# Next pass's x and second-layer weights held back by one-column writes on GpSimd, in a banded-attention and two-layer fp32 kernel

## The chip, the cores and the metric

The kernel runs on one core of a Trainium2 chip. The metric is the device time of one execution in microseconds (us); the median of three runs of the kernel before is 960.06 us (960.06, 960.06, 960.84). One further execution was profiled. Engines are named as in the profile: PE is TensorE's matmuls and PEld its weight loads, DVE is VectorE, ACT is ScalarE, POOL is GpSimd, SP is SyncE, which here only issues DMAs. Each engine runs its own list of instructions in order.

## The reference

q, k, v and the output are float32, the weights are float64. For 4 batches and 8 heads of 576 positions and 64 channels, a causal attention with a band of 64 positions is computed; its output is read as x with 2304 tokens and 512 channels; then come two feed-forward layers:

```
scores = where(0 <= i - j < 64, q @ k.T / 8, -1e9)
x = softmax(scores) @ v                                # 2304 x 512
g = x @ w_gate; x = (g * sigmoid(g) * (x @ w_val)) @ w_out     # 1536 wide
h = x @ w_in;  out = maximum(0.01 * h, h) @ w_out2             # 2048 wide
```

The float64 weights arrive as pairs of 32-bit words and are made float32 on the chip.

## The kernel before, in words

**Numbers.** Each float32 operand of a product is split into a high part (a rounded copy, written by ACT) and a low part (operand minus high part, written by DVE, or by POOL for the activations). Every product then takes three matmuls: high·high, high·low and low·high. `split` (lines 273 to 275) does it for weights and for x, `halves` (lines 635 to 644) for the second layer's activations, with the low part on POOL (line 644).

**First layer.** Tokens go in six blocks (`BLOCKS`, line 51): block 0 and block 5 are 512 tokens wide, blocks 1 to 4 are 320 wide. A block has 12 steps (`step1`, line 539), one for each 128 columns of w_gate and w_val (block 0 has 24, as its tokens go in two halves of 256): product `pg` on PE, tanh on ACT (line 549), `th` on DVE (line 550), product `pv`, `th` again on DVE (line 557), high part g0 on ACT (line 559), low part g1 on POOL (line 560), and then, one step later, `out1` adds g times w_out into four PSUM accumulators. `pg` and `pv` share two PSUM buffers. Attention for the next block runs between the steps, from a plan of slots; a step is three slots, so blocks 1 to 5 have 36 slots each and block 5 begins at slot 216. At the end of a block its x goes to a DRAM buffer, x2d (line 537).

**The second layer's weights** are prepared during the first layer. There are 16 portions of this work, 8 times `ready2` (line 311) and 8 times `ready2o` (line 324), in turn. Each loads two 512 KB pieces (`narrow`, line 257: a DMA by SP into a `raw` buffer, then ACT line 265 and DVE lines 266 and 267 make float32 of it), takes four sums or differences on DVE, splits its seven half-tiles in four calls of `keep2` and stores them in DRAM. All of it goes through the pool `rawp` with three buffers. The portions are handed out at equal distances over slots 92 to 216 (lines 583 to 585), that is, before block 5.

**Second layer.** The two products are done with seven-product (Strassen-Winograd) schemes on halves, over three passes of 768 tokens; a pass has 8 units, so there are 24 units (`units`, line 340; the loop is at line 731). A unit has seven products of 6 matmuls of 384 columns (`product`, line 617: 42 matmuls in the PSUM tiles pw, px, py), whose sums DVE forms (lines 765, 790, 801 to 824), a leaky ReLU on ACT (line 749), the splits of seven operands, and 63 matmuls of 256 columns for the unit before it (`part_y`, line 662), which DVE adds into SBUF sums (line 659; line 657 copies instead of adding in the first unit of a pass). At the end of a pass `finish` and `total` (line 693) put these sums together and store them.

**The next pass's x** comes from x2d. `load_x2(i, part)` (line 397) loads two tiles and issues four subtractions and five splits, `finish_x2` (line 419) four more splits: for the two parts together 8 subtractions and 14 splits, so 22 DVE instructions a pass. It is called for pass 0 in steps 4, 6 and 7 of block 5, and for passes 1 and 2 at the end of units 2 and 4 and in unit 7 of the pass before.

**What sets the order.** The program does not give each engine's order directly. `prio(slot)` sets a priority for what is written next, and a scheduler with a timing model of its own builds the order of each engine from data dependences, free buffers and these priorities. An instruction that is written late with a late priority is still placed early when its data and buffers are there and its engine is free in that model.

Of the kernel before, what the change touches and what calls it, by code (L numbers as in the profile page):

```python
# [27 lines left out]
def banded_attention_moe_moe(  # L28
# [228 lines left out]
    def narrow(src):  # L257

        raw = rawp.tile([P, 512, 2], I32, tag="raw", name="raw")
        flat = raw.rearrange("p f two -> p (f two)")  # L260
# [47 lines left out]
    def two(t):  # L308
        return t.rearrange("p (k n) -> p k n", k=2)

    def ready2(fp):
        x, y = (two(narrow(w2_in[:, f * 2 * P:f * 2 * P + 2 * P].rearrange("(c p) f -> p c f", p=P)))
# [11 lines left out]
    def ready2o(fp):  # L324
        x, y = (two(narrow(w2_out[f * P:f * P + P, :])) for f in (2 * fp, 2 * fp + 1))
# [66 lines left out]
    def split_x2(i, part, k, src):  # L392
        t = two(entry((0, 1, 2, 3, 8, 9), 2 * HALF, place[i][k, part]))
        split(t[:, 0], t[:, 1], src)
        X2[i, part, k] = t

    def load_x2(i, part):

        t0 = PASSES[i]
        r = []  # L400
        for c in (part, part + 2):
            r.append(rawp.tile([P, 2 * HALF], F32, tag="raw", name="x2raw"))
            nc.sync.dma_start(out=r[-1], in_=x2d[c * P:(c + 1) * P, t0:t0 + 2 * HALF])
        b11, b12 = r[0][:, 0:HALF], r[0][:, HALF:2 * HALF]
        b21, b22 = r[1][:, 0:HALF], r[1][:, HALF:2 * HALF]
        t1, t2, t3 = (inb[:, HALF * j:HALF * j + HALF] for j in range(3))
        t4 = (e0, pT)[part].rearrange("p t j -> p (t j)")[:, 0:HALF]
        nc.vector.tensor_tensor(t1, b12, b11, op=ALU.subtract)
        nc.vector.tensor_tensor(t2, b22, t1, op=ALU.subtract)
        split_x2(i, part, A11, b11)  # L410
        split_x2(i, part, S2, t2)
        split_x2(i, part, S1, t1)
        nc.vector.tensor_tensor(t3, b22, b12, op=ALU.subtract)
        nc.vector.tensor_tensor(t4, b21, t2, op=ALU.subtract)
        split_x2(i, part, A12, b21)
        split_x2(i, part, S3, t3)
        x2src[i, part] = (b22, t4)

    def finish_x2(i):
        for j, k in enumerate((S4, A22)):  # L420
            for part in range(2):
                split_x2(i, part, k, x2src[i, part][j])
# [116 lines left out]
    def step1(slot, blk, cols, f, first, last):  # L539
# [20 lines left out]
        nc.gpsimd.tensor_tensor(g[1][:, :n], th, f32(g[0][:, :n]), op=ALU.subtract)  # L560
        reach(slot + 1.4)
# [21 lines left out]
    begin2 = FIRST[1] + 20  # L583
    every = (FIRST[NBLK - 1] - begin2) / NP2
    todo2 = [(begin2 + every * (i + h / 2), fn, i) for i in range(NP2) for h, fn in enumerate((ready2, ready2o))]
    for blk in range(1, NBLK):
        for f in range(NF1):
# [6 lines left out]
            if blk == NBLK - 1:  # L594
                if f in (4, 6):
                    prio(slot - 6)
                    load_x2(0, f // 2 - 2)
                if f == 7:
                    prio(slot - 6)
                    finish_x2(0)  # L600
# [92 lines left out]
    def total(r):  # L693

        s, s1 = f32(sums(r)), f32(sums1())
        for k in (0, 2, 4):
            nc.gpsimd.tensor_tensor(s[:, k], s[:, k], s[:, 1], op=ALU.add)
        nc.vector.tensor_tensor(s1[:, 1, r], s1[:, 1, r], s[:, 0], op=ALU.add)
        nc.vector.tensor_tensor(s1[:, 0, r], s1[:, 0, r], s[:, 2], op=ALU.add)
        return [(s[:, 3], s1[:, 1, r]), (s[:, 4], s1[:, 0, r])]  # L700
# [30 lines left out]
    for n, (i, fp) in enumerate(units):  # L731
# [51 lines left out]
        leaky(t["c"], pw)  # L783
        halves(n, A11, t["c"])
        y(y2, 0)
# [46 lines left out]
        if n + 1 < LAST and i + 1 < len(PASSES) and e in (2, 4):  # L832
            prio(slot - 2)
            load_x2(i + 1, e // 2 - 1)
# [31 lines left out]
```

## Time and profile before

| | value |
|---|---|
| median of three runs | 960.06 us |
| profiled execution, own time | 961.76 us |
| its span, first to last instruction | 960.0 us |
| mean granted TensorE clock | 0.988 of full speed |
| PE busy | 926.4 us, 97% of the span |
| DVE busy | 660.8 us, 69% |
| ACT busy | 465.4 us, 48% |
| POOL busy | 320.7 us, 33% |

By the stores of x to DRAM the six blocks end at about 178, 251, 329, 407, 485 and 584 us; the second layer runs from there to the end, its first products already between the last steps of block 5. A window's count of matmuls is read beside its busy time, since an engine with pipelined instructions looks busy in the profile also where it works at half speed.

### The profile page before, as it was taken

Reading aid. Unit: us, or ns where it says so; the run is one execution under the profiler, and the core shown is the slowest. Engines: PE = TensorE matmul, PEld = TensorE weight load, DVE = VectorE, ACT = ScalarE, POOL = GpSimd, SP = SyncE. Lnnn points to the kernel's source line nnn. Section 1 sums busy time; section 2 is a strip of 40 time slices with the busy share of each in tenths; the row PEclk is TensorE's granted clock in tenths of the full one; section 3 lists DMA queues with packets and bytes.
Section 4 is the critical chain, followed back from the end, with each engine's and each line's share of the span. In section 5 each row is a group of like instructions: output and inputs, shape, how many; then the busy total and the mean of one; then the engine's idle time right before and its main releaser. Section 6 shows DMA issues by size and latency. Waiting matters only on the chain.

```text
span 960.0 us, 18655 instructions
## 1 busy us (share of the span) xinstructions
PE 926.4 (97%) x6573; PEld 880.2 (92%) x6573; DVE 660.8 (69%) x1563; ACT 465.4 (48%) x1194; POOL 320.7 (33%) x343
## 2 busy tenths in 40 slices
PE   7898999999999999999999999899989999999998
PEld 5787999999999999999988889799979999999997
DVE  5788885656756765663324115988889878898786
ACT  6976654545655555564423115434443435344341
POOL 1012331111111111111111115465557655765565
PEclk8999999999999999999999999999989999999999
DMA  8777765765766656573010527777447775487752
GB/s 208 222 209 229 226 174 173 231 202 160 238 185 199 216 156 197 188 224 66 17 45 1 197 77 233 234 235 248 147 152 238 250 250 166 145 264 247 246 165 77
DMA packets 193900, 176.08 MB, mean 183 GB/s; under 512 B 114576, under 2 KB 142224, under 8 KB 193808
## 3 DMA queue, kind: packets, MB, share of 16 engines
q1 hardware_dynamic: 193808, 174.90, 59.7%
q8 instruction: 52, 0.85, 0.4%
q14 instruction: 40, 0.33, 0.1%
HBM read 135.00 MB, written 39.85 MB: 182 GB/s over the span
## 4 chain that ended last, share of the span: by engine, by line
PE 59%; DVE 18%; DMA 14%; ACT 4%; issue 3%; SPq 2%; POOL 0%; DVEq 0%; ACTq 0%
PE y L665 11%; PE pg L507 9%; PE acc L507 9%; PE pv L507 9%; PE px L622 6%; PE yc L665 4%; PE pw L622 4%; PE py L622 4%; DMA raw<-in_moe_w_out_dram 3%; DMA raw<-in_moe_w_gate_dram 3%; DMA raw<-in_moe_w_in_dram 3%; DVE u L267 2%; DVE space L275 2%; DVE space L659 2%; DMA o<-hl 2%
## 5 line engine op out<-in xcount | busy, mean ns | idle before, releaser
L560 POOL TENSOR_TENSOR g<-th,g 128x320 fp32r<-128x320 f32 (+2 forms) x84 | 79.5, 946 | 465.2 <-ACT g L559 459.3
L507 PE MATMUL pg<-x,w 128*128 128x320 f32 (+2 forms) x1008 | 174.6, 321 | 9.5 <-DVE th L550 5.6
L507 PE MATMUL pv<-x,w 128*128 128x320 f32 (+2 forms) x1008 | 173.3, 320 | 2.9 <-DVE st L219 1.4
L507 PE MATMUL acc<-g,w 128*128 128x320 f32 (+2 forms) x1008 | 170.0, 316 | 0.4 <-POOL g L560 0.4
L507 PEld LDWEIGHTS pg<-x,w 128*128 128x128 f32 x1008 | 150.0, 191 | 19.7 <-DVE th L550 7.8
L507 PEld LDWEIGHTS pv<-x,w 128*128 128x128 f32 x1008 | 150.9, 191 | 11.3 <-DVE th L557 2.5
L507 PEld LDWEIGHTS acc<-g,w 128*128 128x128 f32 x1008 | 149.9, 189 | 6.9 <-POOL g L560 0.6
L665 PE MATMUL y<-space,g 128*128 128x256 f32 x1035 | 152.2, 287 | 3.2 <-DVE space L657 1.5
L665 PEld LDWEIGHTS y<-space,g 128*128 128x128 f32 x1035 | 142.1, 194 | 5.4 <-DVE space L657 2.7
L659 DVE TENSOR_TENSOR space<-y,space 128x512 f32<-128x512 f32 (+1 forms) x180 | 104.0, 594 | 24.7 <-PE y L665 23.5
L550 DVE SCALAR_TENSOR_TENSOR th<-th,pg 128x320 f32<-128x320 f32 (+2 forms) x84 | 41.3, 492 | 92.4 <-ACT th L549 92.3
L644 POOL TENSOR_TENSOR g<-t,g 128x384 fp32r<-128x384 f32 x71 | 77.4, 1091 | 53.5 <-ACT g L643 39.0
L622 PE MATMUL px<-space,space 128*128 128x384 f32 x432 | 90.0, 337 | 4.7 <-DVE u L765 2.8
L622 PEld LDWEIGHTS px<-space,space 128*128 128x128 f32 x432 | 74.2, 189 | 6.4 <-DVE u L765 3.2
L559 ACT CAST g<-th 128x320 fp32r<-128x320 f32 (+2 forms) x84 | 39.1, 466 | 74.2 <-DVE th L557 74.0
L265 ACT ACTIVATE u<-raw 128x512 f32<-128x512 f32 x68 | 46.2, 683 | 59.0 <-DMA raw<-in_moe_w_in_dram 27.6
L266 DVE TENSOR_SCALAR raw<-raw 128x512 int32<-128x512 int32 x68 | 32.0, 471 | 53.6 <-DMA raw<-in_moe_w_in_dram 24.2
L549 ACT ACTIVATE th<-pg 128x320 f32<-128x320 f32 (+2 forms) x84 | 36.9, 439 | 65.3 <-PE pg L507 63.0
L665 PE MATMUL yc<-space,g 128*128 128x256 f32 x414 | 66.0, 282 | 0.8 <-DVE space L657 0.8
L644 POOL TENSOR_TENSOR g<-c,g 128x384 fp32r<-128x384 f32 x47 | 50.1, 1066 | 49.4 <-ACT g L643 45.8
L622 PE MATMUL py<-space,space 128*128 128x384 f32 x288 | 64.8, 341 | 0.6 <-ACT t L773 0.6
L622 PE MATMUL pw<-space,space 128*128 128x384 f32 x288 | 64.6, 339 | 0.0
(137 smaller groups left out, 1456.7 us busy)
## 6 DMA issues: line engine op xcount, KB each, us to landing
space<-o SPq DMA_DIRECT2D x147, 256.0 KB, 3.4
space<-a SPq DMA_DIRECT2D x140, 256.0 KB, 3.5
raw<-in_moe_w_out_dram SPq DMA_DIRECT2D x28, 512.0 KB, 5.1
a<-hl SPq DMA_DIRECT2D x24, 512.0 KB, 2.8
o<-hl SPq DMA_DIRECT2D x24, 512.0 KB, 3.2
raw<-in_moe_w_in_dram SPq DMA_DIRECT2D x16, 512.0 KB, 5.8
raw<-in_moe_w_gate_dram SPq DMA_DIRECT2D x12, 512.0 KB, 5.3
raw<-in_moe_w_val_dram SPq DMA_DIRECT2D x12, 512.0 KB, 4.2
```

Source lines behind the costliest of these rows:

```text
L265: nc.scalar.activation(u, f32(high), AF.Prelu, scale=EXP_SCALE, alpha=NEGATIVE)
L266: nc.vector.tensor_single_scalar(low, low, 29, op=ALU.logical_shift_right)
L267: nc.vector.scalar_tensor_tensor(out=ui, in0=ui, scalar=3, in1=low, op0=ALU.logical_shift_left, op1=ALU.bitwise_or)
L507: nc.tensor.matmul(ps, lhsT=w(a, c), rhs=x(b, c), start=(start and n == 0), stop=(stop and n == 3 * len(cs) - 1), skip_group_check=True)
L549: nc.scalar.activation(th, pg, AF.Tanh, scale=0.5)
L550: nc.vector.scalar_tensor_tensor(out=th, in0=th, scalar=1.0, in1=pg, op0=ALU.add, op1=ALU.mult)
L559: nc.scalar.copy(g[0][:, :n], th)
L560: nc.gpsimd.tensor_tensor(g[1][:, :n], th, f32(g[0][:, :n]), op=ALU.subtract)
L622: nc.tensor.matmul(ps, lhsT=A2[n, k][:, a, c * P:c * P + P], rhs=X2[i, c, k][:, b], start=start and m == 0, stop=m == 5, skip_group_check= ...
L644: (lo or nc.gpsimd).tensor_tensor(g[:, 1], src, f32(g[:, 0]), op=ALU.subtract)
L659: nc.vector.tensor_tensor(f32(dst), ps, f32(dst), op=ALU.add)
L665: nc.tensor.matmul(ps, lhsT=g[:, a, r * P:r * P + P], rhs=O2[n, k][:, b], start=start and m == 0, stop=m == 2, skip_group_check=True)
```

## The change

A one-column copy on POOL, `wait_for_mark`, writes the first column of a tile from the result of a given step (the "mark"). The instruction or DMA that fills the tile for real must come after it, as it writes the same memory. The mark is g1 of the newest step in the first layer (line 560) and the leaky ReLU's output c of the newest unit in the second (line 783 before the change).

- The raw loads of `ready2` and `ready2o` get such a write: two in each portion, 32 in all.
- The portions are handed out anew: 10 at equal distances over slots 92 to 216 and 6 in block 5, at slots 219, 224, ... 244.
- `load_x2` becomes `x2_part` in three pieces of three DVE instructions. For passes 1 and 2 the pieces go to units 1 to 6 of the pass before, one in each unit, and each of the three subtractions or splits in a piece gets a one-column write: 36 in all. The loads of x and `finish_x2` have none. For pass 0 all of it goes to step 5 of block 5, without such writes.
- In `total`, three POOL additions of 256 columns become one DVE addition of 768 columns, and two DVE additions become POOL additions.

```diff
+    mark = [None]
+    def wait_for_mark(tile):
+        nc.gpsimd.tensor_copy(tile, mark[0])
-    def narrow(src):
+    def narrow(src, gated=False):
         raw = rawp.tile([P, 512, 2], I32, tag="raw", name="raw")
+        if gated:
+            wait_for_mark(f32(raw)[:, 0, 0:1])
...
-        x, y = (two(narrow(w2_in[:, f * 2 * P:f * 2 * P + 2 * P].rearrange("(c p) f -> p c f", p=P)))
+        x, y = (two(narrow(w2_in[:, f * 2 * P:f * 2 * P + 2 * P].rearrange("(c p) f -> p c f", p=P), True))
...
-        x, y = (two(narrow(w2_out[f * P:f * P + P, :])) for f in (2 * fp, 2 * fp + 1))
+        x, y = (two(narrow(w2_out[f * P:f * P + P, :], True)) for f in (2 * fp, 2 * fp + 1))
...
+    def split_x2(i, part, k, src, gated):
         t = two(entry((0, 1, 2, 3, 8, 9), 2 * HALF, place[i][k, part]))
+        if gated:
+            wait_for_mark(t[:, 0, 0:1])
         split(t[:, 0], t[:, 1], src)
...
+    def x2_part(i, part, piece, gated):
...
+        def less(t, a, b):
+            if gated:
+                wait_for_mark(t[:, 0:1])
+            nc.vector.tensor_tensor(t, a, b, op=ALU.subtract)
+        if piece == 0:
+            less(t1, b12, b11)
+            less(t2, b22, t1)
+            split_x2(i, part, A11, b11, gated)
+        elif piece == 1:
+            less(t3, b22, b12)
+            split_x2(i, part, S2, t2, gated)
+            split_x2(i, part, S1, t1, gated)
+        else:
+            less(t4, b21, t2)
+            split_x2(i, part, A12, b21, gated)
+            split_x2(i, part, S3, t3, gated)
...
         nc.gpsimd.tensor_tensor(g[1][:, :n], th, f32(g[0][:, :n]), op=ALU.subtract)
+        mark[0] = f32(g[1][:, 0:1])
...
-    begin2 = FIRST[1] + 20
-    every = (FIRST[NBLK - 1] - begin2) / NP2
-    todo2 = [(begin2 + every * (i + h / 2), fn, i) for i in range(NP2) for h, fn in enumerate((ready2, ready2o))]
+    begin2, last2 = FIRST[1] + 20, FIRST[NBLK - 1]
+    todo2 = [begin2 + (last2 - begin2) * i / 10 for i in range(10)] + [last2 + 3 + 5 * i for i in range(6)]
+    todo2 = [(at_, (ready2, ready2o)[i % 2], i // 2) for i, at_ in enumerate(todo2)]
...
-                if f in (4, 6):
-                    prio(slot - 6)
-                    load_x2(0, f // 2 - 2)
-                if f == 7:
-                    prio(slot - 6)
+                if f == 5:
+                    prio(slot - 6)
+                    for part in range(2):
+                        for piece in range(3):
+                            x2_part(0, part, piece, False)
                     finish_x2(0)
...
-        for k in (0, 2, 4):
-            nc.gpsimd.tensor_tensor(s[:, k], s[:, k], s[:, 1], op=ALU.add)
-        nc.vector.tensor_tensor(s1[:, 1, r], s1[:, 1, r], s[:, 0], op=ALU.add)
-        nc.vector.tensor_tensor(s1[:, 0, r], s1[:, 0, r], s[:, 2], op=ALU.add)
+        three = s[:, 0:5:2]
+        nc.vector.tensor_tensor(three, three, s[:, 1:2].to_broadcast([P, 3, 256]), op=ALU.add)
+        nc.gpsimd.tensor_tensor(s1[:, 1, r], s1[:, 1, r], s[:, 0], op=ALU.add)
+        nc.gpsimd.tensor_tensor(s1[:, 0, r], s1[:, 0, r], s[:, 2], op=ALU.add)
...
         leaky(t["c"], pw)
+        mark[0] = t["c"][:, 0:1]
         halves(n, A11, t["c"])
+        if i + 1 < len(PASSES) and 0 < e < NP2 - 1:
+            prio(slot - 2)
+            x2_part(i + 1, (e - 1) // 3, (e - 1) % 3, True)
+            prio(slot)
...
-        if n + 1 < LAST and i + 1 < len(PASSES) and e in (2, 4):
-            prio(slot - 2)
-            load_x2(i + 1, e // 2 - 1)
```

## Rows read from the trace of the kernel before

**Rows 1.** The page's first part: busy time, share of the span and number of instructions of each engine (PE is TensorE's matmuls, PEld its weight loads, DVE VectorE, ACT ScalarE, POOL GpSimd).

```profile
PE 926.4 (97%) x6573; PEld 880.2 (92%) x6573; DVE 660.8 (69%) x1563; ACT 465.4 (48%) x1194; POOL 320.7 (33%) x343
```

**Rows 2.** Windows of 20 us in the second layer. Columns: from:to, length, busy us of PE, PEld, DVE, ACT and POOL with the number of instructions in brackets, granted TensorE clock, DMA share, GB/s.

```profile
600.00:620.00 20.00, 16.28 (x90) 14.33 (x88) 20.00 (x35) 9.02 (x20) 7.41 (x7) 0.91 0.76 253
620.00:640.00 20.00, 19.81 (x144) 19.81 (x145) 18.76 (x35) 9.43 (x21) 14.61 (x13) 1.00 0.71 213
...
680.00:700.00 20.00, 20.00 (x143) 19.96 (x142) 19.52 (x34) 11.60 (x26) 10.13 (x9) 1.00 0.60 181
700.00:720.00 20.00, 16.23 (x88) 15.18 (x87) 17.52 (x32) 7.73 (x18) 10.14 (x11) 0.83 0.43 136
720.00:740.00 20.00, 18.98 (x134) 18.59 (x134) 17.92 (x32) 7.53 (x17) 14.26 (x15) 1.00 0.70 205
740.00:760.00 20.00, 20.00 (x144) 20.00 (x142) 18.26 (x34) 8.47 (x18) 14.99 (x15) 1.00 0.86 288
...
840.00:860.00 20.00, 19.41 (x132) 18.89 (x131) 17.94 (x31) 9.69 (x20) 13.83 (x15) 1.00 0.82 263
```

**Rows 3.** Waits of PE, first in 590 to 625 us, then (after the dots) in 690 to 725 us: who waited for whom, us in total, times, longest.

```profile
PE y L665 <- DVE space L657: 1.5, 1, 1.5
PE px L622 <- DVE t L820: 1.2, 1, 1.2
...
PE px L622 <- DVE u L765: 2.2, 1, 2.2
```

**Rows 4.** Timeline of DVE, then of PE, at the first hole, and the same at the second. Columns: start, length, engine, line, operation, out<-in, shape, count, and in square brackets the idle time before it and who ended it.

```profile
605.52 1.35 DVE L275 TENSOR_TENSOR space<-inb,space 128x384 fp32r<-128x384 f32 x1
606.79 0.68 DVE L657 COPY space<-y 128x512 f32<-128x512 f32 x1
607.39 0.54 DVE L275 TENSOR_TENSOR space<-inb,space 128x384 fp32r<-128x384 f32 x1
...
607.53 3.96 PE L665 MATMUL y<-space,g 128*128 128x256 f32 x18 [1.52 <-DVE space L657]
...
708.76 0.54 DVE L414 TENSOR_TENSOR pT<-x2raw,inb 128x384 f32<-128x384 f32 x1
709.23 0.55 DVE L765 TENSOR_TENSOR u<-px,t 128x384 f32<-128x384 f32 x1
...
709.83 1.31 PE L622 MATMUL px<-space,space 128*128 128x384 f32 x6 [2.25 <-DVE u L765]
```

**Rows 5.** DVE's splits alone (line 275) in 595 to 622 and in 691 to 712 us, the columns being from:to, length, busy us (count), clock, DMA share, GB/s; then DVE's subtractions on the next pass's x in 595 to 622 us, with ns min/median/max.

```profile
595.00:622.00 27.00, 8.29 (x10) 0.94 0.80 269
691.00:712.00 21.00, 8.02 (x10) 0.98 0.59 190
...
L408 DVE TENSOR_TENSOR inb<-x2raw x3: 547/580/960, 595.7 to 621.1; 128x384 f32<-128x384 f32 x3
L409 DVE TENSOR_TENSOR inb<-x2raw,inb x2: 547/548/548, 600.6 to 611.4; 128x384 f32<-128x384 f32 x2
L413 DVE TENSOR_TENSOR inb<-x2raw x2: 548/958/1367, 601.1 to 611.9; 128x384 f32<-128x384 f32 x2
```

**Rows 6.** Wider windows, columns as in rows 2.

```profile
180.00:440.00 260.00, 255.38 (x1935) 246.36 (x1934) 164.66 (x510) 144.68 (x431) 36.15 (x40) 1.00 0.65 196
440.00:480.00 40.00, 40.00 (x311) 38.93 (x310) 14.90 (x57) 17.95 (x58) 5.25 (x6) 1.00 0.15 28
480.00:580.00 100.00, 100.00 (x451) 83.52 (x450) 26.20 (x44) 21.74 (x40) 16.32 (x13) 1.00 0.23 77
862.00:935.00 73.00, 73.00 (x520) 73.00 (x519) 59.45 (x108) 31.29 (x66) 42.28 (x41) 1.00 0.69 221
```

**Rows 7.** Timeline of SP's DMA issues: the first portion of the second layer's weights (its loads), the loads of the next portion, and the last portion's loads and last store.

```profile
112.02 4.80 SPq L261 DMA_DIRECT2D raw<-in_moe_w_in_dram  x2
133.25 0.76 SPq L261 DMA_DIRECT2D raw<-in_moe_w_out_dram  x1
...
402.29 1.28 SPq L261 DMA_DIRECT2D raw<-in_moe_w_out_dram  x2
422.31 0.40 SPq L306 DMA_DIRECT2D o<-hl  x1
```

**Rows 8.** Timeline of DVE at the end of the last block, columns as in rows 4.

```profile
574.60 0.69 DVE L550 SCALAR_TENSOR_TENSOR th<-th,pg 128x512 f32<-128x512 f32 x1 [5.81 <-ACT th L549]
576.63 0.69 DVE L557 SCALAR_TENSOR_TENSOR th<-th,pv 128x512 f32<-128x512 f32 x1 [1.34 <-PE pv L507]
```

**Rows 9.** Lines of DVE on a portion of the second layer's weights, whole span: line, engine, operation, out<-in, shape, count, busy us, mean ns of one, idle before and who ended it.

```profile
L266 DVE TENSOR_SCALAR raw<-raw 128x512 int32<-128x512 int32 x68 | 32.0, 471 | 53.6 <-DMA raw<-in_moe_w_in_dram 24.2 <-DMA raw<-in_moe_w_out_dram 23.0 <-DMA raw<-in_moe_w_gate_dram 4.8
L267 DVE SCALAR_TENSOR_TENSOR u<-u,raw 128x512 int32<-128x512 int32 x68 | 48.9, 721 | 4.7 <-ACT u L265 4.4
L315 DVE TENSOR_TENSOR sums<-u 128x256 f32<-128x256 f32 x8 | 3.9, 492 | 0.1
L275 DVE TENSOR_TENSOR hl<-sums,hl 128x512 fp32r<-128x512 f32 x32 | 22.2, 700 | 8.3 <-ACT hl L274 7.6
```

**Rows 10.** Lines of POOL and DVE, columns as in rows 9: a one-column write, and additions of line 697 and 698.

```profile
L122 POOL MEMSET rooms<- 128x1 f32 x8 | 0.4, 94 | 0.0
L697 POOL TENSOR_TENSOR space<-space 128x256 f32<-128x256 f32 x27 | 21.9, 830 | 3.6 <-DVE space L659 2.6 <-PE yc L665 1.0
...
L698 DVE TENSOR_TENSOR space<-space,space 128x256 f32<-128x256 f32 x6 | 5.9, 1015 | 0.0
```

More of the change, by code (lines that the diff above doesn't have):

```diff
@@ L390, in banded_attention_moe_moe @@
     X2, x2src = {}, {}
-    def split_x2(i, part, k, src):
+    def split_x2(i, part, k, src, gated):
         t = two(entry((0, 1, 2, 3, 8, 9), 2 * HALF, place[i][k, part]))
+        if gated:
+            wait_for_mark(t[:, 0, 0:1])
         split(t[:, 0], t[:, 1], src)
         X2[i, part, k] = t
[L397 to L405, printed above, removed]
+    def x2_part(i, part, piece, gated):
         t1, t2, t3 = (inb[:, HALF * j:HALF * j + HALF] for j in range(3))
         t4 = (e0, pT)[part].rearrange("p t j -> p (t j)")[:, 0:HALF]
[L408 to L417, printed above, removed]
+        t0 = PASSES[i]
+        if piece == 0:
+            r = []
+            for c in (part, part + 2):
+                r.append(rawp.tile([P, 2 * HALF], F32, tag="raw", name="x2raw"))
+                nc.sync.dma_start(out=r[-1], in_=x2d[c * P:(c + 1) * P, t0:t0 + 2 * HALF])
+            x2src[i, part] = r[0][:, 0:HALF], r[0][:, HALF:2 * HALF], r[1][:, 0:HALF], r[1][:, HALF:2 * HALF], t4
+        b11, b12, b21, b22, _ = x2src[i, part]
+        def less(t, a, b):
+            if gated:
+                wait_for_mark(t[:, 0:1])
+            nc.vector.tensor_tensor(t, a, b, op=ALU.subtract)
+        if piece == 0:
+            less(t1, b12, b11)
[9 more added lines that the diff above has]
+            split_x2(i, part, S3, t3, gated)
     def finish_x2(i):
@@ L421, in finish_x2 @@
             for part in range(2):
-                split_x2(i, part, k, x2src[i, part][j])
+                split_x2(i, part, k, x2src[i, part][3 + j], False)
     jobs = []
```

## The prediction

> **What bounds the kernel now.** I read the page's engine shares first. PE is busy for 97% of the span [rows 1], so whatever is to be won is a stretch in which PE does less than it could. Busy time alone doesn't show that; the number of matmuls in equal windows does, and these windows were the second view. In the second layer a window of 20 us holds 144 matmuls where all is well. It holds 90 at 600 us, 88 at 700, 134 at 720 and 132 at 840 [rows 2]. At 144 in 20 us the missing ones are worth 54/144 x 20 = 7.5 us, 7.8, 1.4 and 1.7 us: 18.4 us together. In the two large holes DVE is busy for 20.00 and 17.52 us of 20, and the granted clock falls to 0.91 and 0.83 as a mean of the window [rows 2], its lower level (1.2 GHz) being granted for a part of it after PE had stood idle.
>
> The third view, the waits of PE, says on whom it waits there: on DVE (line 657, 820, 765) [rows 3]. The fourth, the timeline, says what DVE does instead. In the first hole a split of the next pass's x (line 275, 1.35 us) stands right before the copy of line 657 for which PE waits 1.52 us. In the second hole line 414, again of the next x, stands before line 765, and PE waits 2.25 us for that [rows 4]. Between 595 and 622 us DVE spends 8.29 us on ten splits. The subtractions cost 0.547 + 0.580 + 0.960 = 2.09 us (line 408), 0.548 + 1.367 = 1.92 us (line 413), and some 0.55 us for each of four more of lines 409 and 414, 2.2 us: 14.5 us of x in 27 us. Between 691 and 712 us it is ten splits, 8.02 us, and their subtractions [rows 5]. The source puts this work into units 2 and 4 of a pass, so the scheduler has placed it earlier, in two heaps: x for pass 1 at the second layer's start, x for pass 2 at the first change of passes.
>
> In the first layer, PE stands idle for 260 - 255.38 = 4.6 us between 180 and 440 us, while weight portions run, and for nothing between 440 and 480 us, when they have ended, nor in 480 to 580 us [rows 6].
>
> **The change part by part.** All terms are made on the profiled execution, whose own time is 961.76 us (span 960.0 us); the median lies 1.7 us below it, and I carry the sum over to the median.
>
> *Portions in blocks 1 to 4.* Portions start some 20 us apart: 112.02, then 133.25; the last takes from 402.29 to 422.31 [rows 7]. So 13 of them lie in the 260 us with 4.6 us of idle time, 0.36 us each. After the change, ten remain before 485 us: 3.6 us, a gain of 1.0. The ends are a gain of 4.6 (all idle time goes) and a loss of 2.6 (a portion costs twice as much). The loss could come from the new write, which waits on POOL for a free raw buffer while line 560 of the next steps queues behind it, and `out1` on PE waits for that.
>
> *Six portions in block 5.* At the same price they would cost 2.2 us. Their cover is wide: DVE idles for 5.81 us ahead of line 550 there [rows 8]. I take 0.5, the ends being 0 and 2.2. If the cover were gone, line 550 would come late, and with it the PSUM buffer for `pg`.
>
> *The first hole.* The x work leaves it, gated to units 1 to 6. But the last portions come near. Their marks are five slots apart, 13.75 us at 99/36 = 2.75 us a slot, while a portion lasted 20 us and the three raw buffers are shared with pass 0's x. The last mark (step 10) comes a step before line 557 of step 11, about 570 us [rows 8]. So the last portion ends at about 591 us if portions follow their marks, and beyond 616 us if they go one behind the other (six times 20 us from the first mark, near 496 us). A portion's DVE work is 2 x 0.471 + 2 x 0.721 + 4 x 0.492 for the sums and at most 4 x 0.700 for the splits: 7.2 us [rows 9]. I take one portion inside the hole in place of 14.5 us of x, and the hole in proportion: 7.5 x (14.5 - 7.2)/14.5 = 3.8 us gained. The ends are 7.5 (none) and -3.7 (three).
>
> *The second hole.* The change of passes at 840 us has the same sums at its end and no heap of x, and costs 1.7 us. So 7.8 + 1.4 - 1.7 = 7.5 us are gained. At most it is 9.2. At least it is what PE waits for line 765 plus what the clock took there, 2.2 + 0.17 x 20 = 5.6 us.
>
> *What the x work costs where it goes.* It isn't less work. A unit is 42 + 63 = 105 matmuls, 105/144 x 20 = 14.58 us. DVE's own work is 59.45/73 of this where there is no x: 11.9 us [rows 6]. Three instructions more, at 14.5/19 = 0.76 us, make 14.2 us, 97% of the unit, in 12 units. The nearest row is the window at 680 us, where DVE is busy for 19.52 of 20 us and PE still does 143 matmuls; that one says 0. The other end is every instruction at the longest of rows 5: 3 x 1.37 = 4.1 us, a unit of 16.0 us, 1.4 us over, 16.7 us in 12 units. I take 2.0, near the row, since at 97% a late instruction is no longer caught up at once.
>
> *The writes themselves.* The nearest row for one column on POOL is 94 ns [rows 10]: 3.4 us for the 36 in the second layer, 3.0 us for the 32 in the first, where POOL is busy for only 36.15 of 260 us. In the second layer they wait for c, and behind them wait lines 644 and 791, which feed the 63 matmuls. POOL has 5 us of 20 free even in the fullest windows [rows 2]. Between 0 and 3.4 us, I take 0.5.
>
> *`total`.* Nine calls. POOL loses 0.83 us in each. DVE exchanges two additions at 1.015 us for one of 768 columns, which the rows bound by 0.68 x 768/512 = 1.0 us (line 657) and 3 x 1.015 = 3.0 us. So 1.0 us less or more on DVE in a call, 3 us at a pass's end, of which the 2.1 us that DVE has free at 840 us hide all but 0.9. For two pass changes: 0, with ends of ±1.8.
>
> Sum: 1.0 - 0.5 + 3.8 + 7.5 - 2.0 - 0.5 = 9.3 us gained. The profiled execution would take 952.5 us, the median 960.06 - 9.3 = 950.8 us.
>
> **The rivals.** *All of it clears.* The portions end before 595 us and DVE at 97% costs nothing: 1.0 + 7.5 + 7.5 = 16.0 us, 944.1 us. For it: 680 to 700 us in rows 2, and 5.81 us of slack in block 5. Against it: the shared raw buffers.
>
> *DVE becomes the bound of 12 units.* This is the slower side. It decides from three x instructions at more than (14.58 - 11.9)/3 = 0.9 us each. Then the units with x are paced by DVE; at 1.37 us the sum is 1.0 - 0.5 + 3.8 + 7.5 - 16.7 - 0.5 = -5.4 us, 965.5 us. For it: line 413 took 1.367 us in one case and 0.548 in the other [rows 5], and line 275 took 1.35 and 0.54 us two microseconds apart [rows 4]; POOL, beside which the long ones run, is busiest in the units' steady part. Against it: the mean of the nineteen is 0.76 us. The Trainium skill (GPSIMD Engine Reference, Key points) says that POOL shares its SBUF interfaces with DVE and that DVE instructions with two SBUF inputs contend with it. By that, all of these instructions are candidates, and so is the 768-column addition; the trace agrees that both lengths occur, and its mean lies below the deciding 0.9 us.
>
> *The portions fill the hole.* Three of them run between 580 and 622 us: -3.7 in place of 3.8, so 1.8 us gained, 958.3 us. For it: 20 us for each portion against marks 13.75 us apart. Against it: in blocks 1 to 4 SP's queue is shared with attention's loads, in block 5 hardly, so the 20 us are an upper price.
>
> *It doesn't hold the work back.* Were the marks early, the heaps would stay where they are and the time with them. The c of unit 1 can't be early, as its product ends at about the time when the heap begins now, so I give this little.
>
> **How the numbers follow.** The forecast has a chance of 0.5, with a range of its own from 945.5 to 956 us. All clear has 0.2, DVE as the bound 0.13, the filled hole 0.13, the rest 0.04. A change within 0.2% (958.1 to 962.0 us) is about what a measurement can't tell from none. Faster: 0.49 + 0.2 + 0.06 + 0.01 = 0.76. Same: 0.01 + 0.05 + 0.01 = 0.07. Slower: 0.17. The range takes in the filled hole and most of all clear, whose best end (4.6 + 7.5 + 9.2 us) would be 938.8 us, and leaves out most of the DVE case: 941 to 962 us.
>
> **What would show it.** Right: no x instruction of line 275 or of a subtraction before unit 1's c, and then three in each of units 1 to 6 and 9 to 14; a window at the first pass change with about 130 matmuls in 20 us and a clock of 1.00; the first window of the second layer between 90 and 144; DVE near 19 of 20 us in units with x and PE still near 143. Wrong: PE waiting on lines 765, 790 or 659 throughout those units; raw loads after 590 us with the first hole as deep as before; PE waiting for line 560 or 644 with a one-column write in front of it on POOL.

## The result, and the profile after

The change makes the kernel slower, by about 1%: 971.26 us as the median of 4 runs (970.53 to 971.84) against 960.45 us for the kernel before beside them, a ratio of 1.0106 [1.0084, 1.0129]. 950.8 us was forecast. The profiled execution took 970.93 us with a span of 969.0 us. Each trace is of one execution, and executions of the kernel before differ by several us, so a gain read from two traces is good to a few us.

The profile after has the same views as before. First, as in [rows 2], windows of the kernel after. Columns: from:to, length, busy us (count) of PE, PEld, DVE, ACT and POOL, granted clock, DMA share, GB/s.

```profile
180.00:480.00 300.00, 299.62 (x2290) 292.69 (x2289) 165.89 (x532) 158.47 (x474) 47.09 (x68) 1.00 0.49 141
480.00:560.00 80.00, 80.00 (x356) 66.37 (x355) 40.96 (x78) 28.79 (x52) 17.21 (x18) 1.00 0.62 220
560.00:640.00 80.00, 59.16 (x308) 53.44 (x307) 53.21 (x92) 32.67 (x66) 29.93 (x35) 0.85 0.77 260
...
580.00:600.00 20.00, 8.53 (x26) 7.20 (x27) 9.86 (x20) 8.30 (x17) 3.13 (x7) 0.59 0.79 264
600.00:620.00 20.00, 12.77 (x67) 12.45 (x67) 12.80 (x22) 8.26 (x17) 8.04 (x7) 0.81 0.88 305
...
700.00:760.00 60.00, 58.12 (x408) 56.76 (x408) 54.94 (x93) 25.00 (x53) 40.13 (x43) 1.00 0.68 212
...
700.00:720.00 20.00, 20.00 (x145) 19.84 (x145) 18.99 (x34) 8.69 (x19) 12.91 (x13) 1.00 0.59 187
740.00:760.00 20.00, 18.12 (x125) 17.17 (x124) 18.61 (x33) 9.10 (x19) 13.42 (x17) 1.00 0.84 268
```

And three wide windows of the kernel before that answer to them, columns the same:

```profile
180.00:480.00 300.00, 295.38 (x2244) 285.30 (x2243) 179.56 (x566) 162.64 (x488) 41.40 (x46) 1.00 0.58 174
...
560.00:640.00 80.00, 76.09 (x442) 70.41 (x442) 53.73 (x90) 33.07 (x69) 37.45 (x32) 0.98 0.59 190
...
700.00:760.00 60.00, 55.21 (x362) 53.77 (x360) 53.69 (x95) 23.73 (x51) 39.39 (x39) 0.94 0.66 209
```

Three stretches account for the difference. From 180 to 480 us PE is busy for 4.2 us more than before. The second hole is gone (145 matmuls at 700 us, where [rows 2] have 88); the pass change itself now lies at 740 us, with 125. The first hole has become a crater: from 560 to 640 us PE does 308 matmuls where it did 442, and the granted clock is 0.59 and 0.81 in the two windows after 580 us. Neither DVE nor any other engine is full there: DVE is busy for 9.86 and 12.80 of 20 us. The DMA engines are busy at 0.79 and 0.88, but in the kernel without the writes on the loads (below) they are at 0.96 and 0.78 in these windows, and PE does 123 and 145 matmuls. So this hole isn't made of work, and its length must be waiting.

Who waits for whom in the crater, in the kernel after from 575 to 615 us: first PE,

```profile
PE py L642 <- ACT c L769: 8.5, 1, 8.5
PE px L642 <- DVE u L815: 7.2, 1, 7.2
```

then ACT and DVE:

```profile
ACT c L769 <- POOL raw L261: 5.5, 1, 5.5
ACT hl L282 <- DMA o<-hl: 4.1, 2, 3.7
...
DVE raw L274 <- DMA raw<-in_moe_w_out_dram: 7.0, 1, 7.0
```

The timeline of the same stretch shows the order (start, length, engine, line, operation, out<-in, shape, count, idle time before and who ended it). L579 makes g1 in the first layer, L261 is the one-column write, L269 a portion's raw load, L314 its stores, L274 its first DVE instruction, L282 and L283 its splits on ACT and DVE, L769 the leaky ReLU that makes c, L815 the addition that makes u3, L642 a product.

```profile
564.49 1.30 POOL L579 TENSOR_TENSOR g<-th,g 128x512 fp32r<-128x512 f32 x1 [3.98 <-ACT g L578]
...
583.67 2.29 PE L642 MATMUL pw<-space,space 128*128 128x384 f32 x6 [0.57 <-ACT t L780]
...
588.63 0.90 SPq L314 DMA_DIRECT2D a<-hl  x2
589.24 0.18 POOL L261 COPY raw<-g 128x1 f32<-128x1 f32 x1 [4.87 <-DVE hl L283]
589.62 4.68 SPq L269 DMA_DIRECT2D raw<-in_moe_w_out_dram  x2
593.75 0.18 POOL L261 COPY raw<-g 128x1 f32<-128x1 f32 x1 [4.33 <-issue]
593.97 0.49 ACT L769 ACTIVATE c<-pw 128x384 f32<-128x384 f32 x1 [5.51 <-POOL raw L261]
...
594.51 2.29 PE L642 MATMUL py<-space,space 128*128 128x384 f32 x6 [8.55 <-ACT c L769]
...
596.22 0.43 DVE L274 TENSOR_SCALAR raw<-raw 128x512 int32<-128x512 int32 x1 [7.04 <-DMA raw<-in_moe_w_out_dram]
...
601.04 1.22 PE L642 MATMUL pw<-space,space 128*128 128x384 f32 x6
...
605.65 0.62 ACT L282 CAST hl<-sums 128x512 fp32r<-128x512 f32 x1 [3.73 <-DMA o<-hl]
606.30 0.69 DVE L283 TENSOR_TENSOR hl<-sums,hl 128x512 fp32r<-128x512 f32 x1 [3.65 <-ACT hl L282]
...
607.67 1.29 DVE L283 TENSOR_TENSOR hl<-u,hl 128x512 fp32r<-128x512 f32 x2 [0.68 <-ACT hl L282]
...
608.89 0.55 DVE L815 TENSOR_TENSOR u<-px,t 128x384 f32<-128x384 f32 x1
...
609.49 2.93 PE L642 MATMUL px<-space,space 128*128 128x384 f32 x8 [7.23 <-DVE u L815]
```

The last portion's mark, the g1 of step 10, is written by 565.8 us. Its first write comes at 589.24 us, after 4.87 us of waiting for a split (L283) of the portion before, which still holds the buffer. So its two loads are issued from 589.62 us on, after the second layer has begun. The second load's write at 593.75 us reads the same g1, whose buffer is one of two that c needs. So c waits for the write, and PE for c: 8.55 us. For the 4.33 us that this write itself stood the profile names nothing ("issue"); in the kernel with a mark of its own (below) the same write waits 4.44 us for a store of the portion before. Then the last portion's splits stand ahead of L815 on DVE, and the splits wait for ACT, which waits for a store to free one of the three buffers that raw, `sums`, `hl` and x share. PE waits 7.23 us more. The two splits at 607.67 us, directly ahead of L815, are extra work of this portion alone: its line 344 calls `keep2` twice more, so it has six calls where the others have four.

The clock comes on top. Six products of 384 columns take 2.29 us at 583.67 and at 594.51 us and 1.22 us at 601.04 us. The first two are at the lower granted level (1.2 GHz; 0.50 in the windows of 2 us from 584 to 600 us). The clock had fallen already before the wait of 8.55 us, after PE had stood idle for 1.84 and 0.57 us between 580 and 583.67 us.

### The profile page after: what moved, and what is told of

The parts are those of the page before. It is cut to its first block, busy times and chain, and to the rows that moved or that the text cites. A ratio compares the mean times of both kernels' runs of the same rounds, so it can differ in the third digit from the quotient of the medians.

```text
span 969.0 us, 18774 instructions
## 1 busy us (share of the span) xinstructions
PE 925.0 (95%) x6573; PEld 881.5 (91%) x6573; DVE 662.6 (68%) x1554; ACT 469.0 (48%) x1194; POOL 336.4 (35%) x402
## 4 chain that ended last, share of the span: by engine, by line
PE 73%; DMA 11%; DVE 8%; issue 2%; ACT 2%; SPq 2%; POOL 1%; POOLq 0%; DVEq 0%; ACTq 0%
PE pg L526 12%; PE y L685 12%; PE pv L526 12%; PE acc L526 12%; PE px L642 7%; PE yc L685 5%; DMA raw<-in_moe_w_gate_dram 4%; PE pw L642 4%; PE py L642 4%; PE s L202 2%; PE pv L244 2%; DMA raw<-in_moe_w_out_dram 1%; DVE u L275 1%; PE pt L233 1%; DMA raw<-in_moe_w_in_dram 1%
## 5 line engine op out<-in xcount | busy, mean ns | idle before, releaser
L579 POOL TENSOR_TENSOR g<-th,g 128x320 fp32r<-128x320 f32 (+2 forms) x84 | 81.5, 970 | 434.9 <-ACT g L578 423.3
L685 PE MATMUL y<-space,g 128*128 128x256 f32 x1035 | 147.5, 283 | 1.0 <-DVE space L677 0.7
L685 PEld LDWEIGHTS y<-space,g 128*128 128x128 f32 x1035 | 138.3, 190 | 2.8 <-DVE space L679 1.0
L569 DVE SCALAR_TENSOR_TENSOR th<-th,pg 128x320 f32<-128x320 f32 (+2 forms) x84 | 41.3, 492 | 93.6 <-ACT th L568 93.4
L642 PE MATMUL px<-space,space 128*128 128x384 f32 x432 | 91.7, 344 | 8.2 <-DVE u L815 7.2
L642 PEld LDWEIGHTS px<-space,space 128*128 128x128 f32 x432 | 76.3, 194 | 9.6 <-DVE u L815 7.8
L642 PE MATMUL py<-space,space 128*128 128x384 f32 x288 | 66.8, 347 | 10.1 <-ACT c L769 8.5
L642 PE MATMUL pw<-space,space 128*128 128x384 f32 x288 | 64.7, 341 | 2.4 <-ACT c L769 1.8
L274 DVE TENSOR_SCALAR raw<-raw 128x512 int32<-128x512 int32 x68 | 31.6, 466 | 47.9 <-DMA raw<-in_moe_w_out_dram 20.3
```

What stands on the lines that cost most here:

```text
L274: nc.vector.tensor_single_scalar(low, low, 29, op=ALU.logical_shift_right)
L569: nc.vector.scalar_tensor_tensor(out=th, in0=th, scalar=1.0, in1=pg, op0=ALU.add, op1=ALU.mult)
L642: nc.tensor.matmul(ps, lhsT=A2[n, k][:, a, c * P:c * P + P], rhs=X2[i, c, k][:, b], start=start and m == 0, stop=m == 5, skip_group_check= ...
L685: nc.tensor.matmul(ps, lhsT=g[:, a, r * P:r * P + P], rhs=O2[n, k][:, b], start=start and m == 0, stop=m == 2, skip_group_check=True)
```

## The experiments

The kernels of one session share their runs of the kernel before, whose medians were 958.41, 958.15 and 957.69 us.

**The x part alone.** The kernel before with `x2_part` in units 1 to 6 and its writes; the portions, pass 0's x and `total` as before.

```diff
-        if n + 1 < LAST and i + 1 < len(PASSES) and e in (2, 4):
...
-            load_x2(i + 1, e // 2 - 1)
...
+        mark[0] = t["c"][:, 0:1]
...
+        if i + 1 < len(PASSES) and 0 < e < NP2 - 1:
...
+            x2_part(i + 1, (e - 1) // 3, (e - 1) % 3, True)
```

> Only the next pass's x is changed for passes 1 and 2 (three pieces a part, one piece in each of units 1 to 6, with their one-column writes); the weight portions, pass 0's x and the sums at a pass's end are as before. Theory A (the last weight portions run into the second layer's start and their waits hold its units up): the heap of x leaves the two holes and nothing new comes, so 945 to 953 us, with some 130 matmuls or more in each 20 us window at the first change of passes. Rival B (the one-column writes and the x instructions on DVE hold the units up): a hole of over 15 us at the second layer's start here too, 965 us or more.

Measured: 945.6 us (944.98 to 945.89), ratio 0.9866 [0.9836, 0.9896]. Its windows, columns as above:

```profile
600.00:620.00 20.00, 19.06 (x137) 19.06 (x138) 19.56 (x36) 9.82 (x21) 12.87 (x17) 1.00 0.79 260
...
640.00:660.00 20.00, 20.00 (x144) 20.00 (x143) 19.08 (x34) 9.06 (x19) 14.10 (x15) 1.00 0.79 257
...
700.00:720.00 20.00, 18.58 (x134) 18.35 (x133) 20.00 (x33) 6.74 (x14) 16.93 (x21) 1.00 0.73 217
720.00:740.00 20.00, 20.00 (x143) 19.95 (x142) 19.61 (x34) 9.82 (x21) 12.99 (x15) 1.00 0.85 285
```

Both holes are gone: 137 matmuls where [rows 2] have 90, 134 where they have 88. At 640 and 720 us DVE is busy for 19.08 and 19.61 of 20 us, and PE does 144 and 143 matmuls beside it. So this part is right: 12.8 us are gained, and the prediction's own terms for it, without a portion in the first hole, make 7.5 + 7.5 - 2.0 - 0.5 = 12.5 us.

**The portions alone.** The kernel before with the portions' writes and new slots and pass 0's x in step 5; the x of passes 1 and 2 and `total` as before.

```diff
-        x, y = (two(narrow(w2_out[f * P:f * P + P, :])) for f in (2 * fp, 2 * fp + 1))
+        x, y = (two(narrow(w2_out[f * P:f * P + P, :], True)) for f in (2 * fp, 2 * fp + 1))
...
+    todo2 = [begin2 + (last2 - begin2) * i / 10 for i in range(10)] + [last2 + 3 + 5 * i for i in range(6)]
```

> Only the weight portions are changed (their one-column writes, the new slots, and pass 0's x in step 5); x of passes 1 and 2 and the sums are as before. Theory A: the hole at the second layer's start is as in the changed kernel or deeper, since the heap of x is there as well, and the hole at the first change of passes stays: 972 to 985 us. Rival B: the portions cost nothing near the second layer, 953 to 961 us.

Measured: 975.85 us (971.68 to 977.37), ratio 1.0176 [1.0138, 1.0214]. PE's waits from 570 to 625 us:

```profile
PE py L642 <- ACT c L769: 8.4, 1, 8.4
PE px L642 <- DVE u L811: 7.1, 2, 6.2
```

The same two waits, without the moved x. The crater belongs to the portions.

**`total` alone.** The kernel before with the new sums only.

```diff
-        for k in (0, 2, 4):
-            nc.gpsimd.tensor_tensor(s[:, k], s[:, k], s[:, 1], op=ALU.add)
...
+        nc.vector.tensor_tensor(three, three, s[:, 1:2].to_broadcast([P, 3, 256]), op=ALU.add)
...
```

> The kernel before with the new sums at a pass's end alone (one DVE addition of 768 columns and two POOL additions in place of two and three). The prediction's term says 0 with ends of 1.8 us either way: 956 to 962 us. If DVE's long addition beside POOL is what costs: 962 us or more.

Measured: 961.55 us (959.75 to 962.77), ratio 1.0038 [1.0023, 1.0053]: 2.2 to 5.1 us slower than the 957.69 us of the kernel before beside it, beyond the ±1.8 of the prediction. That 961.55 us lies in the expected 956 to 962 us is luck: that range was counted from 960.06 us. At the change of passes at 840 us PE does 115 matmuls where [rows 2] have 132, with a clock of 0.91 in place of 1.00:

```profile
840.00:860.00 20.00, 18.19 (x115) 17.71 (x114) 15.33 (x26) 6.43 (x14) 13.33 (x14) 0.91 0.75 238
```

There DVE waits for a store of the finished sums before it copies new ones over them, and PE waits 1.81 us for this copy:

```profile
853.02 0.69 DVE L657 COPY space<-yc 128x512 f32<-128x512 f32 x1 [2.46 <-DMA out_dram<-space]
```

Such waits for a store also occur without the new sums (1.92 us at 735.15 us in the kernel before), so that they are the price is likely, but not shown.

The three parts measured by themselves are -12.8, +17.4 and +3.9 us against their own runs of before, 8.5 us together; the whole measures 10.8 us. Within their intervals that agrees; an interplay of a few us can't be excluded.

**Portions without their writes.** The kernel after, its slots kept, the 32 writes on the portions' loads left out.

```diff
-        x, y = (two(narrow(w2_out[f * P:f * P + P, :], True)) for f in (2 * fp, 2 * fp + 1))
+        x, y = (two(narrow(w2_out[f * P:f * P + P, :])) for f in (2 * fp, 2 * fp + 1))
```

> The changed kernel with its new slots for the weight portions, but without the one-column writes on their loads. Theory A in the form that the write is what holds the last portions back: the scheduler places them early again, 945 to 955 us. Theory A in the form that the slots alone do it: the last portions stay where they are, 965 to 973 us. Rival B: 965 to 973 us.

Measured: 944.96 us (944.47 to 945.43), ratio 0.986 [0.9831, 0.989]. 32 writes cost 971.26 - 944.96 = 26 us in these slots (24 us by the two ratios, as the medians are of different sessions). The slots alone hold only three portions back: the loads of the first 13 start from 111.7 to 340.1 us, and the last three at 508.2, 523.6 and 544.2 us. No portion is left in the second layer:

```profile
580.00:600.00 20.00, 19.00 (x123) 18.67 (x122) 17.01 (x22) 11.61 (x25) 17.13 (x17) 1.00 0.96 327
600.00:620.00 20.00, 20.00 (x145) 20.00 (x144) 19.55 (x37) 9.49 (x20) 12.26 (x18) 1.00 0.78 255
```

**The writes kept, the slots of before.** The kernel after with the 16 portions at before's equal distances.

```diff
-    todo2 = [begin2 + (last2 - begin2) * i / 10 for i in range(10)] + [last2 + 3 + 5 * i for i in range(6)]
+    todo2 = [(begin2 + every * (i + h / 2), fn, i) for i in range(NP2) for h, fn in enumerate((ready2, ready2o))]
```

> The changed kernel with the 16 weight portions at the even slots of the kernel before (all before block 5), their one-column writes kept. Theory A: no portion is near the second layer, so the some 23 us of the changed kernel's hole go: 945 to 953 us. Rival B: as the changed kernel, 965 to 973 us.

Measured: 956.17 us (953.25 to 958.01), ratio 0.9973 [0.9951, 0.9995]. That is in neither of the two ranges expected. The crater is gone (131 matmuls at 600 us), but blocks 1 to 4 pay: from 180 to 480 us PE is busy for 289.43 us, against 297.88 without the writes. POOL does wait there with writes for buffers that earlier portions still hold, and PE's longest waits are for DVE:

```profile
POOL raw L261 <- DVE hl L283: 13.7, 7, 3.7
POOL raw L261 <- DMA a<-hl: 6.0, 3, 2.3
...
PE pg L526 <- DVE th L569: 5.8, 6, 1.7
```

No wait of PE is put down to POOL in this stretch: 7.3 us are put down to DVE and 3.1 us to ACT, which work through the portions in order. In one such case DVE waits for a portion's load right ahead of L569, and PE waits behind it:

```profile
400.22 0.43 DVE L274 TENSOR_SCALAR raw<-raw 128x512 int32<-128x512 int32 x1 [1.83 <-DMA raw<-in_moe_w_in_dram]
...
401.10 2.02 PE L526 MATMUL pg<-x,w 128*128 128x320 f32 x12 [1.74 <-DVE th L569]
```

Portions start 17.9 us apart here in the mean (16 from 220.53 to 488.60 us). In the kernel after it is 25.8 us (ten from 220.74 to 453.29 us), and PE is busy for 299.62 us there. That the distance, and so the number of portions in the stretch, decides fits these kernels; the share of the writes' own waits in it isn't shown.

**A mark of its own.** In the kernel after, each portion copies the mark into a tile of its own first, so that its writes read that and not g1's buffer. One suspect, the wait of c for g1's buffer, is taken away.

```diff
+    def own_mark():
+        m = marks[:, nmark[0] % 4:nmark[0] % 4 + 1]
+        nmark[0] += 1
+        nc.gpsimd.tensor_copy(m, mark[0])
+        mark[0] = m
...
+                own_mark()
                 fn(i)
```

> The changed kernel, in which each weight portion first copies the mark's column into a tile of its own (one more one-column copy on POOL a portion), and its writes read that copy. Theory A1 (the largest stall of PE, 8.4 to 8.5 us for line 769, comes since c takes the buffer of the g1 that a portion's held write still has to read): that stall goes, and with the clock that falls after it 9 to 14 us, so 957 to 962 us. Theory A2 (the portions' loads and stores, for which ACT and DVE wait in order, make the hole by themselves): 967 to 973 us.

Measured: 973.47 us (971.8 to 973.78), ratio 1.0147 [1.0122, 1.0171]: nothing won. c comes at 587.13 us instead of 593.97, as it should, but the waits of PE only change their names:

```profile
PE px L652 <- DVE u L795: 9.2, 1, 9.2
PE px L652 <- DVE u L825: 6.4, 1, 6.4
```

DVE (lines ten higher here) now stands still for the portion itself:

```profile
DVE hl L292 <- ACT hl L291: 10.0, 5, 4.0
DVE raw L283 <- DMA raw<-in_moe_w_out_dram: 8.4, 1, 8.4
```

DVE works in order: it stands at the portion's first instruction until the load has come, and the unit's addition waits behind it. So c's shared buffer is one door to the crater, and not its cause. The cause is that the last portion is still on its way when the second layer starts; the kernels with no portion there (above and below) have no crater.

**Late portions closer.** The kernel after with the six late portions three slots apart, not five, so that the last mark is handed out ten slots earlier.

```diff
-    todo2 = [begin2 + (last2 - begin2) * i / 10 for i in range(10)] + [last2 + 3 + 5 * i for i in range(6)]
+    todo2 = [begin2 + (last2 - begin2) * i / 10 for i in range(10)] + [last2 + 3 + 3 * i for i in range(6)]
```

> The changed kernel with the six late portions three slots apart (219 to 234) and not five (219 to 244), with their one-column writes. Theory S (the slots say when the last portion ends): it ends some 27 us earlier, before the second layer, and 945 to 953 us come out. Theory C (the portions follow one another through the three raw buffers, some 17 us each, and the slots say nothing there): the last one still loads after 575 us, and 960 to 973 us come out.

Measured: 963.87 us (962.96 to 964.9), ratio 1.0057 [1.0036, 1.0077]. The last loads start at 552.0 and 578.6 us, the last one only 11 us earlier than in the kernel after, though its mark is now the g1 of step 6 and not of step 10. Its first write, at 577.20 us, waits 4.36 us for a split of pass 0's x, whose loads came in between through the same three buffers. So the chain through the buffers sets the end, not the marks alone. The crater is smaller (393 matmuls from 560 to 640 us), but PE now loses time inside block 5 as well (busy for 74.89 us from 480 to 560), where POOL waits with writes ahead of L579. PE's waits from 520 to 625 us:

```profile
PE acc L526 <- POOL g L579: 5.6, 2, 5.1
PE px L642 <- DVE u L815: 4.5, 1, 4.5
```

**Three late portions.** The kernel after with 13 portions over blocks 1 to 4 and three in block 5, all with their writes.

```diff
-    todo2 = [begin2 + (last2 - begin2) * i / 10 for i in range(10)] + [last2 + 3 + 5 * i for i in range(6)]
+    todo2 = [begin2 + (last2 - begin2) * i / 13 for i in range(13)] + [last2 + 3 + 5 * i for i in range(3)]
```

> The changed kernel with 13 portions evenly over slots 92 to 216 and three in block 5 (219, 224, 229), all with their one-column writes. Theory A: the last portion is done by some 560 us, the hole is gone: 945 to 955 us, the rest of it being what closer portions cost in blocks 1 to 4 (the even kernel lost some 10 us there against the kernel without writes on the loads). Rival (the writes on the loads cost wherever they are): 955 to 962 us.

Measured: 946.9 us (945.88 to 948.29), ratio 0.9874 [0.985, 0.9898]. The last loads start at 492.7, 509.0 and 527.8 us, and there is no crater:

```profile
580.00:600.00 20.00, 19.99 (x125) 19.50 (x123) 16.03 (x21) 12.15 (x26) 15.11 (x16) 1.00 0.91 317
600.00:620.00 20.00, 19.01 (x137) 19.01 (x138) 19.55 (x36) 9.75 (x21) 12.90 (x17) 1.00 0.79 261
```

In blocks 1 to 4 the portions are 20.3 us apart, and PE is busy for 294.95 us from 180 to 480 us, between the kernel with 17.9 and the one with 25.8 us. So neither the write nor portions in block 5 are dear by themselves: dear are writes on portions that end in the second layer, and, less, writes on portions too close together.

**The x part without its writes.** As the x part alone, but the 36 writes left out.

```diff
-            x2_part(i + 1, (e - 1) // 3, (e - 1) % 3, True)
+            x2_part(i + 1, (e - 1) // 3, (e - 1) % 3, False)
```

> As x_only (the next pass's x alone, in pieces), but without the 36 one-column writes: the pieces are only written into units 1 to 6 of the program. If the writes are what holds the work back: the scheduler places it early again, the holes come back in part, 952 to 961 us. If the place in the program is enough: 944 to 948 us.

Measured: 957.36 us (955.28 to 960.23), ratio 0.9986 [0.9969, 1.0003]. The holes are back:

```profile
600.00:620.00 20.00, 18.18 (x104) 16.38 (x104) 20.00 (x37) 8.96 (x20) 8.80 (x8) 0.93 0.76 247
...
700.00:720.00 20.00, 16.84 (x106) 16.24 (x105) 18.44 (x32) 7.92 (x17) 14.60 (x15) 0.91 0.37 107
```

The place in the program is worth nothing that can be seen, the writes 957.36 - 945.6 = 11.8 us. DVE starts on x at 592.09 us in this kernel, near the 595.7 us of [rows 5], and 19 of its instructions on x have started by 622 us. With the writes DVE starts no later (593.01 us, behind unit 1's c of 589.34 us), but only nine have started by then, three behind each c: the writes spread the heap out.

**Two combinations.** The x part with the new sums; and the portions without writes with pass 0's x back in steps 4, 6 and 7.

```diff
+        three = s[:, 0:5:2]
+        nc.vector.tensor_tensor(three, three, s[:, 1:2].to_broadcast([P, 3, 256]), op=ALU.add)
...
```

> x_only with the new sums at a pass's end: the next pass's x in pieces with its one-column writes, the weight portions as in the kernel before. With the sums at 0, as x_only: 944 to 947 us. If the new sums are worth something at the two changes of passes: 942 to 944 us.

```diff
-                if f == 5:
+                if f in (4, 6):
...
+                    for piece in range(3):
+                        x2_part(0, f // 2 - 2, piece, False)
+                if f == 7:
...
```

> The changed kernel without the writes on the portions' loads and with pass 0's x in steps 4, 6 and 7 as before. The slots of the portions are the only difference to best2: 943 to 947 us if they only say how far portions can be placed ahead; below 943 us if fewer portions in blocks 1 to 4 leave PE less idle there.

Measured: 946.46 us (943.02 to 949.6), ratio 0.9881 [0.9859, 0.9903], and 946.58 us (942.95 to 949.19), ratio 0.9879 [0.9858, 0.9899]. Neither can be told from the x part alone, so beside it the price of the new sums isn't to be seen, nor any effect of pass 0's place in block 5. Five versions lie within 944.96 to 946.9 us, below both kernels: the x part alone, the portions without writes, three late portions, and these two.

## Why the prediction was wrong

**The step that failed is *The first hole*.** It set one portion's 7.2 us of DVE work in place of 14.5 us of x and the hole in proportion: +3.8 us, with -3.7 as the worst end. Three steps of it failed at once. The hole was priced by busy time, but what decides is how long an engine that works in order stands before an instruction whose operand isn't there: DVE idles 7.04 us in front of L274 for a load and 3.65 us in front of L283 for a split that waits for a store. Second, the portion was to follow its mark and end at 591 us; its loads began at 589.62 us, because raw, `sums`, `hl` and x take turns in three buffers. Its mark was there by 565.8 us. The shared buffers were named, but only as a rival. Third, the write reads a tile whose buffer c needs, which wasn't seen at all: a copy of the mark is a reader, and a reader holds the buffer. With a mark of its own this third wait goes, and no time is won by it, so the first two carry the loss. The 7.2 us were short as well: the last portion has six calls of `keep2`, not the four that were counted, and the two more take 1.29 us on DVE. What the sum took for the x alone held: with the x part alone PE does 493 matmuls from 560 to 640 us, 51 more than before, 7.1 us of the 7.5. Measured over 560 to 640 us the term is 442 - 308 = 134 matmuls at 144 in 20 us: -18.6 us.

The sentence that would show the forecast wrong, "raw loads after 590 us with the first hole as deep as before", came true (the second of the last portion's loads is issued behind its write of 593.75 us), with 7.5 + 18.6 = 26.1 us missing where 7.5 were missing before.

***The second hole*: right, as far as one execution of each tells.** +7.5 us were forecast, between 5.6 and 9.2. In the kernel after, 408 matmuls stand in 700 to 760 us, 46 more than before: 46/144 x 20 = 6.4 us. With the x part alone, where pass change and windows lie as before, it is 134 + 143 for 88 + 134: 55/144 x 20 = 7.6 us. The traced execution of the kernel before is one of its longer ones (961.76 us); with the new sums alone, where x is placed as before, the same windows hold 108 and 131 matmuls, and against those it is 38/144 x 20 = 5.3 us.

***What the x work costs where it goes*: no cost is seen in the windows.** With the x part alone DVE is at 19.08 of 20 us and PE at 144 matmuls, and from 640 to 700 us PE does 430, as before. The medians (12.8 us gained for two holes of 15.0 us) don't rule the 2.0 us out. **The rival *DVE becomes the bound*** asked for more than 0.9 us for each x instruction. In that kernel's second layer the 41 of them take 34.4 us from 600 to 830 us, 0.84 us each, so the point was not reached, though not by much. The first and the last of the eight groups that make this sum (columns as in [rows 9]):

```profile
L283 DVE TENSOR_TENSOR space<-x2raw,space 128x384 fp32r<-128x384 f32 x11 | 9.9, 897 | 0.4 <-ACT space L282 0.4
...
L423 DVE TENSOR_TENSOR pT<-x2raw,inb 128x384 f32<-128x384 f32 x2 | 1.2, 588 | 1.4 <-POOL pT L261 1.3
```

The Trainium skill (GPSIMD Engine Reference, Key points) has POOL and DVE share SBUF interfaces, with DVE instructions of two SBUF inputs contending. The trace agrees that the same split takes 0.55 or 1.37 us, and all 16 of the 41 that take over 0.9 us run beside an instruction of POOL; but 19 of the other 25 do so too for a part of their time, so that POOL makes them long isn't shown. Here the long ones are too few.

***Portions in blocks 1 to 4*: +1.0 was too little.** From 180 to 480 us PE gains 299.62 - 295.38 = 4.2 us, near the end of 4.6 that was given; in the four kernels that have portions, pass 0's x and first layer as before (the x part alone, the same without writes, `total` alone, the first and the third together) PE is busy for 296.38 to 297.44 us there, so 2.2 to 4.2 us. The cause was half seen: it is the distance, or the number that lie in the stretch. At 25.8 us from one to the next PE stands for 0.4 us there; at 17.9 us it is busy for 297.88 - 289.43 = 8.5 us less than in the kernel without the writes. The loss that the prediction feared, PE waiting for the g1 that POOL makes late, isn't among PE's waits there; it comes up in block 5 of the kernel with late portions closer (5.6 us). Whether the moved x of pass 0 has a share in the gain wasn't tried.

***Six portions in block 5*: right up to 560 us** (80.00 of 80 us, with 356 matmuls for 361, about 1 us), wrong behind it, where the sixth of them runs into the second layer.

***The writes themselves*: wrong in kind.** 94 ns were taken from a fill; the copies take 183 ns in the median, 282 ns in the mean on raw (columns as in [rows 9], the kernel after):

```profile
L261 POOL COPY raw<-g 128x1 f32<-128x1 f32 x32 | 8.1, 282 | 26.5 <-DVE hl L283 12.1 <-DVE space L283 6.2 <-issue 4.3
```

Their own 8.1 us on POOL are cheap. What can be dear is the waiting: POOL stood still for 26.5 us in front of them, and c waited 5.51 us behind one. Ahead of the 36 x writes it stands for 3.0 us at most in all.

***`total`*: outside its ends.** Alone it costs 2.2 to 5.1 us, where ±1.8 was given. The 768-column addition takes 1.39 us in the mean in that kernel (948 to 1777 ns), inside the 1.0 to 3.0 that its rows bounded. So the size held; what was missed lies in what waits at a pass's end, and which wait it is isn't shown. Why it isn't seen beside the x part wasn't tried.

By windows the terms nearly add up: +4.2 (180 to 480 us), -1.1 (480 to 560: five matmuls of 512 columns at 227 ns), -18.6 (560 to 640), +6.4 (700 to 760), and 13 matmuls fewer in the rest (420 for 430 at 640 to 700 us, 1266 for 1269 at 760 to 940), -1.8: -10.9 us, where the profiled executions differ by 970.93 - 961.76 = 9.2 us.

The rival ***The portions fill the hole*** had the place right and said 958.3 us; its mechanism was DVE's busy time again, and so its price was a fifth of the true one. *It doesn't hold the work back* is refuted: without the writes the x heaps return, and the first 13 portions start 109 to 187 us earlier, the last three 45 to 50 us.

## What to carry to other kernels

A write that makes one piece of work wait for another costs next to nothing where its engine, the buffer it writes and the buffer it reads are free when it comes; ask of each of the three who is queued behind it, and until when. Price late work by its last load and store and by what stands behind it on engines that work in order, not by its busy time. Holding work back can pay only if it is still done before the bound engine's next phase begins, and if there is a hole that it made: holding back the x won 11.8 us. Holding back the portions won nothing as a whole in any kernel here: three late ones with writes came within 2 us of the kernel without writes on the loads (946.9 and 944.96 us), and six cost 24 to 26 us.

## What was not expected of the hardware

- With DVE busy for 19.08 and 19.61 of 20 us PE does 144 and 143 matmuls, as with 18.26 us; the row at 680 us of [rows 2] was no exception.
- The granted clock is at its lower level in a part of the crater (0.59 and 0.81 as means of two windows). It had fallen after idle times of 1.84 and 0.57 us, stayed there through the wait of 8.55 us, and the same six products take 2.29 us at it and 1.22 us at the full level, so a stall is paid a second time.
- A one-column copy on POOL takes 183 ns in the median, but up to 2602 ns in this trace, and twice a one-column fill of 94 ns [rows 10].
